# Batch sums moved to earlier steps, and a subtraction of hidden blocks moved from VectorE to GpSimd, in a Strassen-like feed-forward kernel

## The chip, the cores and the metric

The kernel runs on one core of a Trainium2 chip. The metric is device time in microseconds (us) of one execution, the median of several. Engines are called as in the profile: PE (TensorE, matrix products), PEld (its weight loads), DVE (VectorE), ACT (ScalarE), POOL (GpSimd) and SP (SyncE, which only issues transfers here). Each takes its own queue of instructions in order; they meet by semaphores.

## The reference, cut to what matters

```python
# x: (8, 8, 512, 64), state: (8, 8, 32, 64); attention both ways
scores = x @ state^T / sqrt(D);  xread = softmax(scores) @ state
scores2 = state @ x^T / sqrt(D); sread = softmax(scores2) @ x
x = concat([xread, sread], axis=2)       # to (B*(512+32), 512) = (4352, 512)
# feed-forward with w_in (512, 2048), w_out (2048, 512)
h = x @ w_in
g = h * cos(h)
out = g @ w_out
```

All is float32. The cost lies in the two large products.

## The kernel before, in words

The tokens' read of the state is never formed. Since xread = a @ state, the kernel multiplies state by w_in first (the tiles `sw`, by `products`), and h of a batch's 512 tokens is then a product with `sw` and the softmax weights `aT`, with 256 instead of 512 terms.

Work goes in steps. A step is one tile: a batch b and one of 16 blocks f of 128 of the 2048 hidden columns, 128 columns by 512 tokens (128 steps for 8 batches, then 16 for the state rows). `step` counts through, `s` is the step within a batch. Two batches form a pair, and its 32 steps are four phases of 8: 0 and 1 in the even batch, 2 and 3 in the odd one. The second product (g @ w_out) of a pair is done with seven block products instead of eight, so blocks of g of different phases are added and subtracted from each other before they are used. `sums` (L658) and `sums2` (L667) do this by `minus` (L577), which puts the subtraction on DVE where it is called with `True` and the pair isn't the first, and on POOL otherwise.

The first product, h, is also done with seven products of half size where `seven` says so (batches from 2 on, phases 0 to 2), for two tiles at a time:

- `halves` (L481) makes four sums of the quarters of `aT`, on DVE, into `aS`, once a batch (L488).
- `sw_sums` (L496) makes four sums of quarters of `sw`, on POOL, for each couple of tiles: t1, t2 and t4 into `swS`, the fourth in place in `sw` (L502).
- `hidden_a` (L519) is the first four products on PE: one of `aT` and `sw` as they are, then one with t2, one with the quarter changed in place, one with t1 (all L507). `hidden_b` (L542) is the other three, one with t4. `sums_a` (L537 to L539) and `sums_b` (L552, L553) add the parts into g's buffer on DVE, after a copy by ACT (L529).
- `gate` to `gate4` then compute h * cos(h): ACT L560 rounds, DVE L563 subtracts, ACT L566 is the sine, DVE L573 multiplies and leaves g.

`swS` and `aS` have one buffer each. The PSUM pool of h has two buffers.

The order is written out by hand: each engine takes its instructions in the order in which the loop over steps (L920 on) issues them. In a step t: `hidden_b` and `sums_b`, or `hidden` (two plain products, L471); `hidden_a` of the couple that begins at the next step, where there is one; the parts of the attention of the next batch that `plan` puts here; the gates; `gate4`; `sums(t)`; more parts; the sums of w_out's blocks; at the end `sw_sums` for the couple that begins at step + 2, with `halves` before it when that couple begins a batch; `sums2(t)`; and the second product of the tile three steps back (`LAG = 3`, L617). So `hidden_a` of a couple is issued one step after its `sw_sums`.

Of the kernel before, what the change touches and what calls it, by code (L numbers as in the profile page):

```python
# [21 lines left out]
def kernel(  # L22
# [15 lines left out]
    NF = Dff // P  # L38
# [144 lines left out]
    def fetch(n):  # L183
        nonlocal n_fetched
        while n_fetched < n:
            dst, src = loads[n_fetched]
            if f64:
                m, w = dst.shape[1:]

                at_, c0 = (n_fetched - 2) % 3, 0  # L190
                if n_fetched < 4:
                    at_, c0 = n_fetched // 2, n_fetched % 2 * 2 * m * w
                if n_fetched >= N_LOADS:
                    at_ = 3 + n_fetched - N_LOADS
                raw = raw_at[at_].bitcast(I32)[:, c0:c0 + 2 * m * w]
                raw = raw.rearrange("p (m f) -> p m f", m=m)
                nc.sync.dma_start(out=raw, in_=src.bitcast(I32))
                raws[n_fetched] = raw.rearrange("p m (f w) -> p m f w", w=2)
            else:
                nc.sync.dma_start(out=dst, in_=src)  # L200
            n_fetched += 1
# [49 lines left out]
    class Attention:  # L251
# [126 lines left out]
        def sums(self):  # L378
            self.reduce1([self.z1[:, j] for j in range(2)], ALU.add)
            self.inverse(self.m1 if self.b == 0 else self.i12)  # L380
# [72 lines left out]
    def part(b, name, *args):  # L453

        if b not in attn:
            attn[b] = Attention(b)
        getattr(attn[b], name)(*args)
        if (name, args) == ("reads", (1,)) and b + 1 < B:
            if b > 0:
                attn[b + 1] = Attention(b + 1)  # L460
                attn[b + 1].load_tokens()
            load_x(b + 1)
# [16 lines left out]
    def seven(t):  # L479
        return t.pair is not None and t.b > 1 and t.phase < 3  # L480

    def halves(b):
        aT = aT_of[b]
        b11, b12 = aT[:, 0, 0:HS], aT[:, 0, HS:S]
        b21, b22 = aT[:, 1, 0:HS], aT[:, 1, HS:S]
        for i, x1, x2 in ((0, b12, b11), (1, b22, aS[:, 0]), (2, b22, b12),
                          (3, b21, aS[:, 1])):
            nc.vector.tensor_tensor(aS[:, i], x1, x2, op=ALU.subtract)  # L488

    def blocks_of(t):  # L490
        sw = sw_of[t.b, P * t.f // WC]
        c = P * t.f % WC
        return [sw[:, j, c + P * r:c + P * r + P] for r in range(2)
                for j in range(2)]

    def sw_sums(t):  # L496
        b11, b12, b21, b22 = blocks_of(t)
        t1, t2, t4 = [swS[:, i] for i in range(3)]
        sub = ALU.subtract
        for o, x1, x2, op in ((t1, b21, b22, ALU.add), (t2, t1, b11, sub),  # L500
                              (t4, b12, t2, sub), (b21, b11, b21, sub)):
            nc.gpsimd.tensor_tensor(o, x1, x2, op=op)  # L502
# [6 lines left out]
    def take_slot(t):  # L509
        t.slot = g_free.pop(0)  # L510
        t.hp = t.g = g_all[:, t.slot, 0:t.n]

    def both(i1, i2):

        d = i2 - i1
        ends = slice(i1, i2 + (1 if d > 0 else -1), d)
        return g_all.rearrange("p t (h s) -> p (t h) s", h=2)[:, ends]
# [31 lines left out]
    def sums_b(t):  # L549
        e, o = 2 * t.slot, 2 * t.second.slot  # L550
        add = nc.vector.tensor_tensor
        add(t.g[:, LO], t.g[:, LO], t.h1[:, LO], op=ALU.add)  # L552
        add(both(o, e + 1), both(o, e + 1),  # L553
            t.h2.rearrange("p (h s) -> p h s", h=2), op=ALU.add)
# [14 lines left out]
    def gate4(t):  # L569
        if not hasattr(t, "slot"):  # L570
            t.slot = g_free.pop(0)
            t.g = g_all[:, t.slot, 0:t.n]
        nc.vector.tensor_tensor(t.g, t.hp, t.q, op=ALU.mult)  # L573
# [3 lines left out]
    def minus(pr, out, a, b, soon=False):  # L577
        engine = nc.vector if soon and pr.n else nc.gpsimd
        engine.tensor_tensor(out, a, b, op=ALU.subtract)  # L579
# [78 lines left out]
    def sums(t):  # L658
        pr, i = t.pair, t.i
        pr.b[t.phase, i] = t  # L660
        if t.phase == 2:
            minus(pr, pr.b[0, i].g, t.g, pr.b[0, i].g, True)
        if t.phase == 3:
            minus(pr, pr.b[0, i].g, t.g, pr.b[0, i].g, True)
            minus(pr, pr.b[2, i].g, t.g, pr.b[2, i].g)
# [99 lines left out]
    def tiles():  # L765
        pr = None
        for b in range(B):
            if b % 2 == 0:
                pr = Pair(b // 2, pr)
            for f in range(NF):  # L770
                t = Tile()
                t.b, t.f, t.pair = b, f, pr
                t.phase, t.i = b % 2 * 2 + f // NH, f % NH
                t.n, t.kn = S, 2
                c = slice(P * f % WC, P * f % WC + P)
                t.lhs = lambda i, b=b, nt=P * f // WC, c=c: (
                    sw_of[b, nt][:, i, c])
                t.rhs = lambda i, b=b: aT_of[b][:, i]
                yield t
        for n in range(NF):  # L780
            t = Tile()
            t.b, t.n_th, t.f = B, n, (n + NH) % NF
            t.pair, t.last_pair, t.phase = None, pr, None
            t.n, t.kn = B * Ns, NK
            cols = slice(P * t.f, P * t.f + P)
            t.lhs = lambda i, cols=cols: w_in[:, i, cols]
            t.rhs = lambda i: sT[:, :, Ns * i:Ns * i + Ns]
            yield t
# [130 lines left out]
    all_tiles = list(tiles())  # L919
    for step, t in enumerate(all_tiles):  # L920
        s = step % NF
        if s == 0 and t.b < B:
            steps = plan(t.b)
        todo = [p[s] if t.b < B else [] for p in steps]

        def go(n):
            for p in todo[n]:
                part(*p)

        last, conv = conv_at.get(step - 1, -1), conv_at.get(step, -1)  # L930
        if step == B * NF + (0 if f64 else 8):
            fetch(N_LOADS + 2)
        if step == 4:
            warm(1, acc[MAIN][0])
        ahead = all_tiles[step + 1:step + 3]
        if seven(t):
            if t.f % 2 == 0:
                hidden_b(t)
                sums_b(t)
        elif step != 1:  # L940
            hidden(t)
        first = len(ahead) > 1 and seven(ahead[0]) and ahead[0].f % 2 == 0
        if first:
            if not seven(t):

                h = t.hp
                take_slot(t)
                nc.scalar.copy(t.g, h)
            hidden_a(*ahead)
        if step == 0:  # L950
            hidden(all_tiles[1])
            warm(3, acc[MAIN][0])
            gate(t)
            gate2(t)
            convert(3, "bcdf")
            convert(4, "1")
            go(0)
        else:
            go(0)
            if step == 5:  # L960
                states(1, acc[SIDE][1])
            if not (seven(t) and t.f % 2):
                gate(t)
            gate2(t)
            if step == 3:
                warm(4, acc[MAIN][0])
                part(0, "products", 1, SIDE)
            if first:
                sums_a(ahead[0])
            go(1)  # L970
            go(3)
            if step == 1:
                convert(4, "bcdf")
            elif last >= 0:
                convert(last, "bcdf")
            if conv >= 0 and not todo[1]:
                convert(conv, "1")
        gate3(t)
        if seven(t) and t.f % 2 == 0:
            gate(t.second)  # L980
        if step == 3:
            part(0, "products_kept", 1, SIDE)
        if later:
            later.pop(0)()
        gate4(t)
        if conv >= 0 and todo[1] and step > 0:
            convert(conv, "1")
        if t.pair is not None:
            sums(t)
        if step == 6:  # L990
            states_kept(1, acc[SIDE][1])
        go(2)
        if conv >= 0:
            convert(conv, "2")
        go(4)
        if step in block_at:
            blocks(*block_at[step])
        for u in all_tiles[step + 2:step + 3]:
            if seven(u) and u.f % 2 == 0:
                if u.f == 0:  # L1000
                    halves(u.b)
                sw_sums(u)
        if t.pair is not None:
            sums2(t)
        while len(line) >= (LAG if step >= 2 * NH else LAG + 1):
            output(line.pop(0))
        line.append(t)
# [32 lines left out]
```

## Time and profile before

| | |
|---|---|
| median of 3 runs | 775.27 us (774.0 to 775.3) |
| profiled execution | 775.59 us |
| its span, first to last instruction | 773.7 us |
| PE busy | 755.5 us, 98% |
| DVE busy | 519.6 us, 67% |
| ACT busy | 316.2 us, 41% |
| POOL busy | 251.1 us, 32% |
| mean granted PE clock | 0.996 of full |

In the views of the profile a line has a start in us, a duration in us, the engine, the line of the kernel, the operation, and output<-input with sizes. `x2` is a number of merged instructions; a float32 product stands as two matmuls. In square brackets stands how long the engine was idle before it and which engine, tile and line released it. A line of the waits reads: who waited <- for whom: us in total, times, longest. The view of stretches gives, for each, its length, the busy time and count of PE, PEld, DVE, ACT and POOL, then the granted PE clock (1.00 is full), the DMA share and GB/s.

### The profile page before, as it was taken

How to read it: one execution, taken by the hardware profiler on the slowest of the kernel's cores; microseconds unless marked ns; L12 is line 12 of the kernel's file. 1: busy time of each engine (PE TensorE's matmuls, PEld its weight loads, DVE VectorE, ACT ScalarE, POOL GpSimd, SP SyncE). 2: the span in 40 equal slices, each digit the busy share in tenths (PEclk: the TensorE clock that was granted, in tenths of full speed). 3: DMA queues.
4: the chain of work that ended last, by engine and by line, in shares of the span. 5: the costliest groups of instructions: out<-in, count | busy, mean ns of one | idle time of the engine just before them, and what ended most of it. 6: DMA issues, size and time to landing. Idle time of an engine off the chain costs nothing.

```text
span 773.7 us, 8418 instructions
## 1 busy us (share of the span) xinstructions
PE 755.5 (98%) x2880; PEld 380.5 (49%) x2880; DVE 519.6 (67%) x858; ACT 316.2 (41%) x523; POOL 251.1 (32%) x262
## 2 busy tenths in 40 slices
PE   8998999999999999999999999999999999999997
PEld 4443444444555554445555554445555554455554
DVE  5778786645896788756886788567877676431431
ACT  3887844422363435333362335332453333212212
POOL 2353278866121210753121111662121105510200
PEclk9999999999999999999999999999999999999999
DMA  8596451050012510340104310330100115000021
GB/s 244 171 276 206 129 90 28 13 96 1 7 21 43 94 25 4 51 87 0 19 10 83 54 28 14 61 62 1 27 1 1 28 28 136 0 0 15 14 42 41
DMA packets 161962, 43.54 MB, mean 56 GB/s; under 512 B 153920, under 2 KB 153920, under 8 KB 161920
## 3 DMA queue, kind: packets, MB, share of 16 engines
q1 hardware_dynamic: 161024, 42.49, 25.2%
q10 hardware_dynamic: 768, 0.39, 0.2%
q8 instruction: 23, 0.38, 0.2%
q0 software_dynamic: 128, 0.13, 0.1%
q14 instruction: 19, 0.16, 0.1%
HBM read 34.08 MB, written 8.91 MB: 56 GB/s over the span
## 4 chain that ended last, share of the span: by engine, by line
PE 82%; DVE 9%; POOL 3%; ACT 3%; issue 1%; DMA 1%; ACTq 0%; SPq 0%; DVEq 0%; POOLq 0%
PE o L617 44%; PE h L507 14%; PE h L471 13%; PE at L319 4%; PE o L737 4%; PE at L409 2%; DVE q L563 1%; POOL g_all L579 1%; DVE g_all L573 1%; ACT q L560 1%; DVE xT L339 1%; PE o L319 1%; POOL swS L502 1%; ACT q L566 1%; DVE i L333 1%
## 5 line engine op out<-in xcount | busy, mean ns | idle before, releaser
L617 PE MATMUL o<-g_all,w_out 128*128 128x512 f32 x512 | 236.4, 598 | 0.3 <-POOL w_out L242 0.3
L617 PE MATMUL o<-g_all,s 128*128 128x512 f32 x384 | 178.9, 602 | 0.0
L579 POOL TENSOR_TENSOR g_all<-g_all 128x512 f32<-128x512 f32 x80 | 113.2, 1436 | 125.2 <-DVE g_all L573 125.2
L617 PEld LDWEIGHTS o<-g_all,w_out 128*128 128x128 f32 x512 | 93.8, 190 | 113.3 <-issue 108.6
L566 ACT ACTIVATE q<-q,halfpi 128x512 f32<-128x512 f32 (+1 forms) x144 | 100.7, 700 | 91.1 <-DVE q L563 90.9
L563 DVE TENSOR_TENSOR q<-q,h 128x512 f32<-128x512 int32 (+1 forms) x69 | 42.9, 622 | 115.6 <-ACT q L560 115.6
L617 PEld LDWEIGHTS o<-g_all,s 128*128 128x128 f32 x384 | 71.5, 192 | 89.2 <-issue 82.9
L471 PE MATMUL h<-aT,sw 128*128 128x512 f32 x224 | 107.0, 601 | 4.8 <-DVE g_all L573 4.3
L560 ACT ACTIVATE q<-g_all 128x512 int32<-128x512 f32 x75 | 46.8, 624 | 143.9 <-DVE g_all L553 143.5
L560 ACT ACTIVATE q<-h 128x512 int32<-128x512 f32 (+1 forms) x69 | 37.7, 546 | 134.3 <-PE h L471 134.2
L563 DVE TENSOR_TENSOR q<-q,g_all 128x512 f32<-128x512 int32 x75 | 54.8, 731 | 30.8 <-ACT q L560 30.8
L471 PEld LDWEIGHTS h<-aT,sw 128*128 128x128 f32 x224 | 41.8, 190 | 60.0 <-issue 45.1
L502 POOL TENSOR_TENSOR swS<-sw 128x128 f32<-128x128 f32 x36 | 17.7, 492 | 150.0 <-PE h L507 110.6
L573 DVE TENSOR_TENSOR g_all<-g_all,q 128x512 f32<-128x512 f32 x75 | 52.9, 706 | 14.4 <-ACT q L566 14.3
L573 DVE TENSOR_TENSOR g_all<-h,q 128x512 f32<-128x512 f32 (+1 forms) x69 | 42.8, 621 | 25.0 <-ACT q L566 24.6
L242 POOL TENSOR_TENSOR w_out<-w_out,s 128x1024 int32<-128x1024 int32 x10 | 23.9, 2395 | 77.5 <-DVE w_out L237 71.3
L502 POOL TENSOR_TENSOR swS<-sw,swS 128x128 f32<-128x128 f32 x36 | 18.9, 524 | 89.6 <-PE h L507 89.1
L507 PE MATMUL h<-aS,swS 128*128 128x256 f32 x144 | 43.4, 383 | 4.6 <-POOL swS L502 2.4
L507 PE MATMUL h<-aS,sw 128*128 128x256 f32 x144 | 43.2, 382 | 1.4 <-POOL sw L502 1.2
L507 PEld LDWEIGHTS h<-aT,sw 128*128 128x128 f32 x144 | 27.4, 190 | 34.4 <-issue 27.7
L507 PE MATMUL h<-aT,sw 128*128 128x256 f32 x144 | 42.8, 379 | 0.0
L579 DVE TENSOR_TENSOR g_all<-g_all 128x512 f32<-128x512 f32 x48 | 33.4, 696 | 1.6
(103 smaller groups left out, 883.9 us busy)
## 6 DMA issues: line engine op xcount, KB each, us to landing
out_dram<-ot SPq DMA_DIRECT2D x132, 64.0 KB, 2.0
g_all<-in_moe_w_out_dram SPq DMA_DIRECT2D x8, 1024.0 KB, 5.1
g_all<-in_moe_w_in_dram SPq DMA_DIRECT2D x6, 1024.0 KB, 5.4
xT<-in_x_dram SPq DMA_DIRECT2D x96, 64.0 KB, 2.5
x_b<-in_x_dram SPq DMA_DIRECT2D x24, 256.0 KB, 4.4
x_b<-in_x_dram SPq DMA_DIRECT2D x16, 128.0 KB, 3.8
g_all<-in_moe_w_in_dram SPq DMA_DIRECT2D x4, 512.0 KB, 6.2
x_b<-in_moe_w_out_dram SPq DMA_DIRECT2D x1, 1024.0 KB, 5.5
```

Source lines behind the costliest of these rows:

```text
L242: nc.gpsimd.tensor_tensor(bits, bits, e, op=ALU.add)
L319: nc.tensor.matmul(out=(to or at)[j][Ns * k:Ns * k + Ns, 0:n], lhsT=w[D * j:D * j + D, self.b, Ns * k:Ns * k + Ns], rhs=r(slice(D * j, D * ...
L471: nc.tensor.matmul(out=t.hp, lhsT=t.lhs(i), rhs=t.rhs(i), start=(i == 0), stop=(i == t.kn - 1))
L502: nc.gpsimd.tensor_tensor(o, x1, x2, op=op)
L507: nc.tensor.matmul(out=out, lhsT=w, rhs=r, start=True, stop=True)
L560: nc.scalar.activation(t.q.bitcast(I32), t.hp, func=ACTF.Copy, bias=0.25)
L563: nc.vector.tensor_tensor(t.q, t.q.bitcast(I32), t.hp, op=ALU.subtract)
L566: nc.scalar.activation(t.q, t.q, func=ACTF.Sin, bias=halfpi, scale=-TWO_PI)
L573: nc.vector.tensor_tensor(t.g, t.hp, t.q, op=ALU.mult)
L579: engine.tensor_tensor(out, a, b, op=ALU.subtract)
L617: nc.tensor.matmul(out=acc[bank][ch], lhsT=w[:, i, P * ch:P * ch + P], rhs=g.g, start=(i == 0), stop=(i == NH - 1))
L737: nc.tensor.matmul(out=acc[MAIN][i], lhsT=t.g[:, P * i:P * i + P], rhs=w_out[:, :, t.f, :], start=(t.n_th == 0), stop=(t.n_th == NF - 1))
```

## The change

Four places change. `halves` of an odd batch (b > 1) is issued in step 14 of the even batch, right after `sums_b`, where it was at the end of that step. `halves` of an even batch is issued at the end of step 11 of the batch before, where it was at the end of step 14. `sw_sums` of the first couple of an even batch is issued in step 13, ahead of `gate4` and `sums` of that step, where it was at the end of step 14. And `minus` of phase 2 loses its `True`, so that in all pairs it goes to POOL.

```diff
+    def new_pair(t):
+        return t.b % 2 == 0 and t.f == 0
+
...
         if t.phase == 2:
-            minus(pr, pr.b[0, i].g, t.g, pr.b[0, i].g, True)
+            minus(pr, pr.b[0, i].g, t.g, pr.b[0, i].g)
...
             if t.f % 2 == 0:
                 hidden_b(t)
                 sums_b(t)
+                if s == NF - 2 and seven(all_tiles[step + 2]):
+                    halves(t.b + 1)
...
         if later:
             later.pop(0)()
+        for u in all_tiles[step + 3:step + 4]:
+            if seven(u) and new_pair(u):
+                sw_sums(u)
         gate4(t)
...
         go(4)
+        for u in all_tiles[step + 5:step + 6]:
+            if seven(u) and new_pair(u):
+                halves(u.b)
         if step in block_at:
             blocks(*block_at[step])
         for u in all_tiles[step + 2:step + 3]:
-            if seven(u) and u.f % 2 == 0:
-                if u.f == 0:
-                    halves(u.b)
+            if seven(u) and u.f % 2 == 0 and not new_pair(u):
                 sw_sums(u)
```

## The prediction

> **What bounds the kernel now.** I read the busy table first, then TensorE's waits, then the timeline around each wait, then the granted clock in narrow windows. Busy share:
>
> ```profile
> PE 755.5 (98%) x2880; PEld 380.5 (49%) x2880; DVE 519.6 (67%) x858; ACT 316.2 (41%) x523; POOL 251.1 (32%) x262
> ```
>
> TensorE (PE) is busy 98% of the 773.7 us span, so an edit can gain only what PE's waits hold, and costs what new waits it makes. PE's waits (us in total, times, longest), those of the seven-product matmuls at L507:
>
> ```profile
> PE h L507 <- POOL swS L502: 2.4, 3, 1.5
> PE h L507 <- DVE aS L488: 2.2, 3, 0.7
> PE h L507 <- POOL sw L502: 1.2, 3, 0.5
> ```
>
> 5.8 us in all: POOL's `sw_sums` at the start of each even batch (2, 4, 6), DVE's `halves` at the start of each odd one (3, 5, 7). PE's timeline at batches 2, 3 and 4:
>
> ```profile
> 168.93 0.59 PE L507 MATMUL h<-aT,sw 128*128 128x256 f32 x2
> 171.00 0.70 PE L507 MATMUL h<-aS,swS 128*128 128x256 f32 x2 [1.47 <-POOL swS L502]
> 171.95 0.70 PE L507 MATMUL h<-aS,sw 128*128 128x256 f32 x2 [0.25 <-POOL sw L502]
> 172.48 0.61 PE L507 MATMUL h<-aS,swS 128*128 128x256 f32 x2
> ...
> 258.51 0.67 PE L507 MATMUL h<-aS,swS 128*128 128x256 f32 x2 [0.73 <-DVE aS L488]
> ...
> 342.40 0.70 PE L507 MATMUL h<-aS,swS 128*128 128x256 f32 x2 [0.46 <-POOL swS L502]
> ```
>
> The four products of a `hidden_a` start 0.43 us apart when nothing is missing, 1.30 from first to fourth. In batch 2 it is 168.93 to 172.48 = 3.55: 2.25 lost, more than the idle column says. The clock after that wait (columns: stretch, us, five busy times, PEclk, DMA):
>
> ```profile
> 172.90:176.30 3.40, 3.40 (x6) 1.54 (x5) 2.81 (x5) 1.00 (x2) 0.56 (x2) 0.50 0.00 0
> ...
> 342.00:346.00 4.00, 3.11 (x11) 1.84 (x12) 3.02 (x6) 2.01 (x5) 2.69 (x4) 1.00 0.03 6
> ```
>
> After 1.72 us of idle in batch 2, PE ran 3.4 us at half clock: 1.7 us more lost. After 0.95 us in batch 4 it didn't. A 1.95 us wait at 73 us was also followed by about 3.4 us at 0.50. So a PE wait of over some bound between 0.95 and 1.72 us costs a further 1.7.
>
> [...] POOL's first sum at 341.12 starts just as the `minus` ahead of it ends (339.39 + 1.77). [...] Here L579 takes a median of 1.28 us on POOL and 0.69 on DVE.
>
> **Part 1: the even batches' sums sooner.** `halves` goes from the end of step 14 of the batch before (between L573 and L563 in DVE's queue) to the end of step 11; `sw_sums` goes to step 13, ahead of six `minus` of POOL. As built, POOL's order is so. That wait goes: 2.25 + 1.7 of clock in batch 2, and in batches 4 and 6 (341.35 to 344.13, 510.90 to 513.68: 2.78 - 1.30) 1.48 each: 6.9 us. Late next would be ScalarE's copy that frees the second h buffer: L948 ends at 342.19, the third product would start at 342.21; nothing. The cost: the first `minus` of step 13 waits for the copies of sw (L445 ends near 332.2) and four sums (2.0), so till 334.2 instead of 333.67. Its reader comes three steps later. POOL is idle 2.7 us before its next, and the 1.6 us of `halves` at step 11 meets DVE idling over 2 us per step (3.14 before the L563 at 330.72). Without that cover they'd cost some 0.5 and 1.6, three times. No DMA moves, no queue of SP is passed.
>
> **Part 2: the odd batches' `halves` sooner**, right after `sums_b` of step 14. PE's group in batch 3 takes 257.19 to 259.45 = 2.26: 0.96 lost, three times 2.9 us. `halves` (257.49 to 259.04, 1.55) now stands ahead of L563 of step 14, which waits 0.75 for ScalarE's L560 anyway: gate and g of that tile come 0.8 later, read three steps on. Nothing. Parts 1 and 2 together: -9.8 us.
>
> **Part 3: phase 2's `minus` from DVE to POOL**: 24 instructions (8 in each of batches 3, 5, 7). DVE sheds 24 x 0.69 = 16.6 us, no gain: DVE isn't the bound. POOL has 24 x 1.4 = 34 us more, of which it has plenty idle. The cost is order. In an even step t of phase 2, POOL's queue now has `minus(t)`, then the four `sw_sums` of tile t+2. `minus(t)` waits for g of tile t (L573), which ends the whole chain behind `hidden_b(t)`: sums, L560, L563, L566, L573. The four sums wait behind it; their readers are the second to fourth products of `hidden_a(t+2)`, and everything else of PE stands behind those. Now POOL does the last sums straight after `hidden_b`. Batch 3, step 0:
>
> ```profile
> 264.29 0.59 PE L507 MATMUL h<-aS,sw 128*128 128x256 f32 x2
> 265.02 0.46 POOL L502 TENSOR_TENSOR sw<-sw 128x128 f32<-128x128 f32 x1
> 267.95 0.69 DVE L573 TENSOR_TENSOR g_all<-g_all,q 128x512 f32<-128x512 f32 x1 [0.27 <-ACT q L566]
> 268.52 0.59 PE L507 MATMUL h<-aS,sw 128*128 128x256 f32 x2
> 268.68 0.69 DVE L579 TENSOR_TENSOR g_all<-g_all 128x512 f32<-128x512 f32 x1
> ```
>
> The sums are ready at 265.48, PE wants the last at 268.52: 3.0 us spare. After the change they can start only once L573 (268.64) and `minus` are done. I take 0.08 for the hop (346.84 + 0.69 to 347.61), 1.4 for `minus` (1.27 to 1.77 seen) and 2.0 for four sums (1.95 by the pitch of undisturbed ones, 2.42 beside a busy DVE): 3.48, bounds 3.3 and 4.3. So ready at 272.12: 3.6 late, and 0.15 for the restart: 3.75. Since hidden_b, chain and the next hidden_a all move with PE, each stall adds and the next comes again. Step 2: L573 ends 277.93, ready 281.41, wanted 278.41: 3.15. Step 4: L573 ends 288.52, less some 0.4 because DVE's `minus` no longer delays L552: 288.1, ready 291.6, wanted 289.51: 2.25. Step 6 has no reader (tile 8 isn't of the seven kind). Batch 3: 9.15, batch 5 repeats it, batch 7 (607.76, 617.05, 627.0 against 607.64, 617.53, 628.63): 8.9. Sum 27.2 us.
>
> And the clock: idle of about 3.3, 2.7 and 1.8 us within each stall, over or at the 1.72 that halved it. A full 3.4 us at half clock costs 1.7; where the slow stretch falls partly in the stall itself, less. I take 1.5, 1.3 and 0.7: 3.5 a batch, 10.5 in all (0 to 15).
>
> **Sum.** 27.2 + 10.5 - 9.8 = +27.9. The profiled execution took 775.59 (773.7 span and 1.9 around it): 803.5. The median, 775.27, is 0.3 below it, which I let stand.
>
> **The rivals.**
> - A, forecast: new waits with clock drops, 803.5.
> - B: the same waits, but the clock holds[...]: 775.6 + 17.4 = 793. For it: 0.95 in two pieces was harmless. Against: 1.72 in two pieces wasn't.
> - C: POOL at its slow prices (4.3 instead of 3.48, 9 x 0.8 = 7) and a full drop everywhere (15.3 - 10.5 = 5): 815. For it: L502 took 0.9 in places. Against: DVE mostly idles while PE waits, and it is beside each other that the two are slow: `halves` took 1.37 and 1.48 instead of 0.42 beside POOL's `minus` at 167 us.
> - D, the other side: g of tile t comes early enough for `minus` and sums to fit before `hidden_a(t+2)` and only the gain stays, 775.6 - 9.8 = 766. It decides where L573 ends 3.5 us before PE's need; now it ends 0.1 before it in step 0, 0.5 in step 2 and 1 in step 4. DVE freed of 0.69 doesn't bring 2.5. With only step 0 late (3 x 5.3) it would be +6, 782.
> - E: the change doesn't do what it says. As built, the order of POOL and DVE shows all three moves, PE's order is unchanged. I give it nothing.
>
> **How the numbers follow.** A 0.72, B 0.12, C 0.09, D 0.04, its mild form at 782 0.03. The range runs from below B, for the low prices of POOL, to C: 790 to 815; beyond lie D and part of C. About 0.2% can be told from no change here. Faster 0.04 (D), within 0, slower 0.96 (A, B, C and the mild form).
>
> **What would show it.** Right: waits of L507 on POOL in batches 3, 5 and 7, nine groups of 2 to 4 us, sum over 20; the waits on L488 and those at batches 2, 4, 6 gone; PEclk of 0.5 for some 3.4 us after most stalls, mean clock from 0.996 to about 0.97; `minus` 104 on POOL and 24 on DVE; in phase 2 each first sum of a POOL group starting as a `minus` ends. Wrong: PE's first product of `hidden_a` in these batches waiting for nothing, L573 of an even tile ending 3 us earlier against `hidden_b` than now, or stalls under 1 us.

## The result and the profile after

The changed kernel takes 803.78 us (median of 4 runs, 802.15 to 806.69) against 774.67 us before (4 runs on the same chip): 1.038 times as long, 95% interval 1.034 to 1.042. The profiled execution took 802.24, its span is 800.4, 26.7 more than before. The forecast was 803.5. That it is so near is partly luck: of the terms of the sum the largest, the stalls, was right to 1 us, and three others were wrong by 2 to 6 us each and cancelled.

Its page, busy time first:

```profile
span 800.4 us, 8434 instructions
...
PE 761.4 (95%) x2880; PEld 381.2 (48%) x2880; DVE 514.3 (64%) x834; ACT 315.2 (39%) x523; POOL 277.1 (35%) x286
```

PE's busy time rose only by 6 us of the 27: it waits. Its waits (us in total, times, longest):

```profile
PE h L512 <- POOL swS L507: 22.2, 10, 3.1
PE h L471 <- DVE g_all L578: 4.8, 4, 1.9
PE h L512 <- POOL sw L507: 2.2, 9, 0.2
...
PE o L622 <- DVE held L635: 1.4, 2, 0.7
...
PE h L512 <- ACT g_all L955: 0.2, 1, 0.2
```

(Lines are numbered anew: L507 is the sums of `sw`, L512 the seven products, L578 the end of the gate, L584 `minus`, L493 `halves`, L622 the second product, L635 DVE's copy of a finished second product, L955 ScalarE's copy that frees a buffer of h, L910 the sums of w_out's blocks.) The waits on `halves` are gone, those on POOL went from 3.6 to 24.4 us. POOL's timeline in batch 3, at the step whose timeline the prediction shows:

```profile
265.69 1.64 POOL L584 TENSOR_TENSOR g_all<-g_all 128x512 f32<-128x512 f32 x1 [13.25 <-DVE g_all L578]
267.29 0.45 POOL L507 TENSOR_TENSOR swS<-sw 128x128 f32<-128x128 f32 x1
267.82 0.45 POOL L507 TENSOR_TENSOR swS<-swS,sw 128x128 f32<-128x128 f32 x1
268.35 0.46 POOL L507 TENSOR_TENSOR swS<-sw,swS 128x128 f32<-128x128 f32 x1
268.77 0.45 POOL L507 TENSOR_TENSOR sw<-sw 128x128 f32<-128x128 f32 x1
```

and PE's, same stretch:

```profile
264.62 0.59 PE L512 MATMUL h<-aT,sw 128*128 128x256 f32 x2
268.33 1.22 PE L512 MATMUL h<-aS,swS 128*128 128x256 f32 x2 [3.11 <-POOL swS L507]
269.34 1.15 PE L512 MATMUL h<-aS,sw 128*128 128x256 f32 x2
```

POOL was idle for 13.25 us, and the sums could have been made within that time: the first thing in its queue was `minus`, and that waited for DVE's L578, which ended at 265.61. `minus` takes 1.64, the sums 1.93, and PE stands. The products then take 1.22 and 1.15 instead of 0.59: the clock had been halved inside the wait, as the view of the stretches has it (PEclk is third from the end):

```profile
268.00:271.40 3.40, 3.07 (x7) 2.27 (x8) 0.44 (x2) 0.99 (x2) 1.14 (x3) 0.50 0.00 0
```

PE issues the same 2880 products in the same order in both kernels, so the start of the k-th product in one trace can be set against the start of the k-th in the other, and each step in the difference, from level to level, is a gain or a loss at its place:

| where | predicted | found in the two traces |
|---|---|---|
| batch 2, first couple: wait and clock | -2.25 - 1.7 | -1.75 - 1.7 |
| batch 2, second couple | 0 | +1.4 |
| batches 4 and 6 | -1.48 each | -1.29 each |
| batches 3, 5, 7, `halves` | -0.96 each | -0.97 each |
| phase 2, step 0 (three times) | 3.75 each | 3.9 each |
| step 2 | 3.15 each | 3.3 each |
| step 4 | 2.25 (2.0 in batch 7) | 2.2 each |
| clock in those stalls | 10.5 | 1.0 + 1.7 + 1.55 = 4.3 |
| phase 3 of batches 3 and 5 | 0 | +0.95 each |
| sum | +27.9 | +26.7 |

### The profile page after: what moved, and what is told of

Same layout as the page of the kernel before. It is cut to its first block, busy times and chain, and to the rows that moved or that the text cites. A ratio compares the mean times of both kernels' runs of the same rounds, so it can differ in the third digit from the quotient of the medians.

```text
span 800.4 us, 8434 instructions
## 1 busy us (share of the span) xinstructions
PE 761.4 (95%) x2880; PEld 381.2 (48%) x2880; DVE 514.3 (64%) x834; ACT 315.2 (39%) x523; POOL 277.1 (35%) x286
## 4 chain that ended last, share of the span: by engine, by line
PE 75%; DVE 10%; POOL 6%; ACT 4%; issue 4%; DMA 1%; DVEq 0%; SPq 0%; POOLq 0%; ACTq 0%
PE o L622 39%; PE h L471 13%; PE h L512 13%; PE o L742 3%; PE at L319 3%; POOL g_all L584 3%; POOL swS L507 2%; DVE g_all L578 2%; PE at L409 2%; DVE g_all L584 1%; DVE q L568 1%; ACT q L571 1%; DVE xT L339 1%; PE o L319 1%; ACT q L565 1%
## 5 line engine op out<-in xcount | busy, mean ns | idle before, releaser
L622 PE MATMUL o<-g_all,w_out 128*128 128x512 f32 x512 | 238.9, 604 | 0.3 <-POOL w_out L242 0.3
L584 POOL TENSOR_TENSOR g_all<-g_all 128x512 f32<-128x512 f32 x104 | 140.4, 1363 | 197.6 <-DVE g_all L578 190.1
L622 PE MATMUL o<-g_all,s 128*128 128x512 f32 x384 | 177.9, 598 | 1.4 <-DVE held L635 1.4
L622 PEld LDWEIGHTS o<-g_all,w_out 128*128 128x128 f32 x512 | 95.1, 192 | 114.4 <-issue 109.5
L622 PEld LDWEIGHTS o<-g_all,s 128*128 128x128 f32 x384 | 70.7, 190 | 90.2 <-issue 82.8
L568 DVE TENSOR_TENSOR q<-q,g_all 128x512 f32<-128x512 int32 x75 | 52.8, 704 | 35.4 <-ACT q L565 35.4
L512 PE MATMUL h<-aS,swS 128*128 128x256 f32 x144 | 45.3, 397 | 22.2 <-POOL swS L507 22.2
L578 DVE TENSOR_TENSOR g_all<-g_all,q 128x512 f32<-128x512 f32 x75 | 54.3, 724 | 14.4 <-ACT q L571 14.4
L578 DVE TENSOR_TENSOR g_all<-h,q 128x512 f32<-128x512 f32 (+1 forms) x69 | 42.8, 621 | 24.5 <-ACT q L571 24.0
L507 POOL TENSOR_TENSOR swS<-sw 128x128 f32<-128x128 f32 x36 | 17.3, 480 | 107.0 <-PE h L512 66.9
L512 PE MATMUL h<-aS,sw 128*128 128x256 f32 x144 | 45.1, 395 | 2.4 <-POOL sw L507 2.2
L512 PEld LDWEIGHTS h<-aT,sw 128*128 128x128 f32 x144 | 27.4, 190 | 34.4 <-issue 28.2
L512 PE MATMUL h<-aT,sw 128*128 128x256 f32 x144 | 42.8, 379 | 0.0
L512 PEld LDWEIGHTS h<-aS,swS 128*128 128x128 f32 x144 | 27.3, 195 | 29.7 <-POOL swS L507 26.2
L507 POOL TENSOR_TENSOR swS<-sw,swS 128x128 f32<-128x128 f32 x36 | 18.3, 507 | 60.8 <-PE h L512 59.6
```

Source lines behind the costliest of these rows:

```text
L512: nc.tensor.matmul(out=out, lhsT=w, rhs=r, start=True, stop=True)
L568: nc.vector.tensor_tensor(t.q, t.q.bitcast(I32), t.hp, op=ALU.subtract)
L622: nc.tensor.matmul(out=acc[bank][ch], lhsT=w[:, i, P * ch:P * ch + P], rhs=g.g, start=(i == 0), stop=(i == NH - 1))
```

## The experiments

All times are medians beside runs of the kernel before on the same chip, which were 774.1 to 775.4. The runs stand on several chips, so a difference of under 1 us between two of them says little. My theory: the whole loss is the order in POOL's queue, `minus` ahead of sums that are due sooner. The rivals: POOL has too much work, or gets in DVE's way; moving the sums has a cost of its own; the parts work only together.

**The moved sums without the move to POOL.** The changed kernel with

```diff
-            minus(pr, pr.b[0, i].g, t.g, pr.b[0, i].g)
+            minus(pr, pr.b[0, i].g, t.g, pr.b[0, i].g, True)
```

> The change with phase 2's minus left on DVE: only the moved halves and sw_sums. Theory (the cost lies in POOL's queue order alone): no waits of PE at the changes of batches, and no new ones in phase 2 of batches 3, 5, 7; from the shifts of PE between the two traces -3.5 in batch 2 (1.2 given back at its second couple), -1.15 each in batches 4 and 6, -0.75 to -0.93 in batches 3, 5, 7: 767.5 us (766 to 769). Rival (moving the sums costs too, they take DVE's or POOL's time from the gates): 774 or more.

Measured 767.12 us, 0.990 of before (0.989 to 0.992). Parts 1 and 2 are a gain, 7.7 us; the rival is out.

**The move to POOL alone.** The kernel before with the opposite edit of that one line.

> The kernel before with phase 2's minus on POOL and nothing else. Theory: all of the loss and none of the gain: stalls of 27.5, phase 3 up by 1.8, four to seven clock drops of 1.5: 810 us (806 to 815). Rival (the loss comes from the two parts together, as PE runs ahead of POOL once its early waits are gone): well under 800.

Measured 807.97 us, 1.044 (1.042 to 1.046). The loss needs nothing of the other parts: 33.1 us alone, 36.7 on top of them, with different numbers of stretches at half clock, of which more below.

**The same work on POOL, in another order.** The changed kernel with

```diff
+        for u in all_tiles[step + 2:step + 3]:
+            if t.phase == 2 and seven(u) and u.f % 2 == 0:
+                sw_sums(u)
         gate4(t)
...
-            if seven(u) and u.f % 2 == 0 and not new_pair(u):
+            if (seven(u) and u.f % 2 == 0 and not new_pair(u)
+                    and t.phase != 2):
                 sw_sums(u)
```

> The changed kernel with all 24 minus on POOL, but in phase 2 the four sums of the next couple are issued ahead of gate4 and minus, so they stand before it in POOL's queue. Theory (order): the nine stalls go, what is left is e1 and phase 3's 1.8: 769.3 us (768 to 771). Rival (POOL has too much to do, or gets in DVE's way): 790 or more, as POOL does the same work.

Measured 769.98 us, 0.993 (0.992 to 0.995): all but 2.9 us of the loss (803.78 to 767.12) is gone with the same 24 `minus` on POOL. Its timeline at the same place of batch 3:

```profile
260.52 0.45 POOL L507 TENSOR_TENSOR swS<-sw,swS 128x128 f32<-128x128 f32 x1 [3.48 <-PE h L512]
260.93 0.46 POOL L507 TENSOR_TENSOR sw<-sw 128x128 f32<-128x128 f32 x1
264.63 1.66 POOL L584 TENSOR_TENSOR g_all<-g_all 128x512 f32<-128x512 f32 x1 [3.24 <-DVE g_all L578]
```

The sums are done at 261.4, 3.2 us before `minus` may even start, and `minus` starts 1.06 us after PE's first product of the group, where it did so 1.07 after it in the changed kernel. So POOL's load and its meeting with DVE are not the cause of the stalls; the order is. What PE still waits for in this kernel:

```profile
PE h L471 <- DVE g_all L578: 4.7, 4, 1.9
PE at L799 <- DVE g_all L119: 1.5, 1, 1.5
PE o L622 <- DVE held L635: 1.4, 2, 0.7
PE h L512 <- POOL swS L507: 1.0, 1, 1.0
```

The 1.0 is that at batch 2's second couple, the L635 that of phase 3; both come below.

**Half of it each.** `i` is the tile within its phase, so its oddness is the step's.

```diff
-            minus(pr, pr.b[0, i].g, t.g, pr.b[0, i].g)
+            minus(pr, pr.b[0, i].g, t.g, pr.b[0, i].g, i % 2 == 0)   # odd moved
+            minus(pr, pr.b[0, i].g, t.g, pr.b[0, i].g, i % 2 == 1)   # even moved
```

> The changed kernel with only the odd tiles' minus of phase 2 on POOL (12 of 24); the even ones stay on DVE. Theory: an odd tile's minus has no sums of its own step behind it and is done before the next couple's may start, so nothing stalls; phase 3 keeps at most half of its loss: 768.5 us (767 to 770). Rival (each minus on POOL costs alike): half of the loss, about 785.

> The changed kernel with only the even tiles' minus of phase 2 on POOL (12 of 24). Theory: all nine stalls and their clock drops: 803 us (800 to 807). Rival (each minus costs alike): about 785.

Measured 768.06 us (0.991, 0.989 to 0.992) with the odd ones moved, 802.26 (1.035, 1.032 to 1.039) with the even ones. Twelve instructions of the same kind and length on the same engine: 1 us over the kernel with none moved, or 35. Only the even ones stand ahead of sums in their own step.

**Products that fill the wait.** The changed kernel with, in `hidden_a`,

```diff
         product_of(t.h1[:, LO], b11, aT_of[t.b][:, 0, LO])
+        for _ in range({2: 3, 4: 2, 6: 1}.get(t.f, 0) if t.phase == 2 else 0):
+            nc.tensor.matmul(out=t.h2, lhsT=ident, rhs=w_in[:, 0, 0:WC],
+                             start=True, stop=True)
```

(their results are overwritten).

> The changed kernel with products that nothing reads (3, 2 and 1 of 0.86 us) behind the first product of hidden_a in steps 2, 4 and 6 of phase 2, inside the wait. Theory (the spread of 802 to 807 is the number of clock drops that the stalls set off): the stalls stay (27.5), no drop in batches 3, 5, 7: 797.8 us, runs within 1 us of each other. Rival (the drops cost nothing beyond the wait, or the spread has another cause): 803 or more, with a spread of 4.

Measured 797.99 us (1.029, 1.028 to 1.031), four runs from 796.58 to 798.58. In batch 3 PE is kept busy, and the next product starts 3.71 us after the first, as it did in the changed kernel:

```profile
263.16 0.59 PE L512 MATMUL h<-aT,sw 128*128 128x256 f32 x2
263.59 2.74 PE L529 MATMUL h<-w_in,ident 128*128 128x512 f32 x6
...
266.87 0.70 PE L512 MATMUL h<-aS,swS 128*128 128x256 f32 x2 [0.54 <-POOL swS L507]
```

Its trace has no half clock in the batches (its mean clock is 0.999, and PEclk is 1.00 from 264 to 272 us and from 278 to 286). PE was given more work and the kernel became 5.8 us faster. Set against the changed kernel's trace, PE gains 1.0, 1.7 and 1.55 us at the three stalls that had half clock there, 1.3 in batch 0, where no filler stands and the drop is missing too, and nothing elsewhere. So the gain is the price of the clock drops, and 4.3 of it is that of the drops in the stalls. The changed kernel's own runs say the same. From the granted clock and the span, the number of 3.41 us stretches at half clock is (1 - clock) x span / 1.705:

| run, us | clock | span | stretches |
|---|---|---|---|
| 802.15 | 0.991 | 800.2 | 4.2 |
| 802.24 | 0.991 | 800.4 | 4.2 |
| 805.32 | 0.987 | 803.4 | 6.1 |
| 806.69 | 0.985 | 804.8 | 7.1 |

Three more stretches, 4.5 us more: 1.5 each. In these four runs the spread goes with the number of clock drops. (In the four runs with filled waits, 2.0 us apart, it does not: the slowest of them, 798.58, has a clock of 1.000.)

Which wait sets one off shows in part. In the changed kernel's trace the half-clock stretches of batches 3 and 5 last 3.413 us each and start at 267.97, 448.87 and 462.53: 180.90 and 13.66 us apart, 53 and 4 times that length. So I cut each of the thirteen traces into windows of that length, placed by its own half-clock stretches, and counted PE's idle time in each window at full clock after the first 12 us. All 11 windows with over 2.5 us idle were followed by half clock, and none with under 1.7; of the 17 with 1.71 to 1.95 eight were, and why those is open. The same stall of 2.55 us at step 2 lay whole in one window in batch 5 (459.11 to 462.53), and the clock fell; in batch 3 a boundary at 281.62 cut it, the windows had 1.6 and 1.2 us idle, and it did not. That the clock goes by such windows is my reading of these counts; no run tested it by itself.

**Batch 2's second couple.** The kernel with `minus` on DVE, and

```diff
-        if step in block_at:
-            blocks(*block_at[step])
         for u in all_tiles[step + 2:step + 3]:
             if seven(u) and u.f % 2 == 0 and not new_pair(u):
                 sw_sums(u)
+        if step in block_at:
+            blocks(*block_at[step])
```

> The changed kernel with phase 2's minus on DVE, and besides with the sums of w_out's blocks behind sw_sums in a step, not ahead. Theory: the wait at batch 2's second couple (1.02 + 0.24 and the restart), which came to light once PE was 3.5 us earlier there, is POOL's block sum of 2.4 us ahead of sw_sums; it goes, 1.2 us off: 766.0 us. Rival (PE then finds the next late thing at once, or the third couple's sums stand behind the block sum instead): 767.1, as without it.

Measured 765.6 us, 0.987 (0.986 to 0.989), 1.5 below the kernel without it; against that kernel's trace PE gains 1.8 at batch 2's second couple and nowhere else after batch 0. What stood ahead of the sums there, in the changed kernel:

```profile
177.62 2.86 POOL L910 TENSOR_TENSOR w_out<-w_out 128x1024 f32<-128x1024 f32 x1
180.44 0.91 POOL L507 TENSOR_TENSOR swS<-sw 128x128 f32<-128x128 f32 x1
...
182.26 0.70 PE L512 MATMUL h<-aS,swS 128*128 128x256 f32 x2 [1.02 <-POOL swS L507]
```

**Phase 3.** In the changed kernel DVE and POOL start their `minus` of phase 3 (L584) together, as here:

```profile
326.59 1.26 POOL L584 TENSOR_TENSOR g_all<-g_all 128x512 f32<-128x512 f32 x1 [0.80 <-DVE g_all L578]
326.62 1.79 DVE L584 TENSOR_TENSOR g_all<-g_all 128x512 f32<-128x512 f32 x1
328.33 0.68 DVE L635 TENSOR_SCALAR held<-o 128x512 f32<-128x512 f32 x1
```

The kernel before, at the like place:

```profile
315.24 0.69 DVE L579 TENSOR_TENSOR g_all<-g_all 128x512 f32<-128x512 f32 x1
315.29 1.78 POOL L579 TENSOR_TENSOR g_all<-g_all 128x512 f32<-128x512 f32 x1 [2.35 <-DVE g_all L573]
```

In the pairs of either kernel that start within 0.05 us of each other, whichever started first ran at its usual 0.69 or 1.27, and the other took 1.77 to 1.80. In the changed kernel POOL is first in 12 of the 24 tiles, the first four of each batch; in the others DVE's is still first or alone, at 0.69. DVE's reads what POOL's `minus` of phase 2 wrote, and in just these 12 DVE takes a semaphore instruction of 0.02 us ahead of it, starts 0.10 after L578 instead of 0.03 (once 0.46), and so comes second. With only the odd tiles moved that instruction stands at the odd ones of the first four, with only the even ones moved at the even ones. L635, which frees the bank of PE's next product (PE waited for it twice, 1.4 us in all), stands behind DVE's `minus`. To turn the order round, the changed kernel with

```diff
             minus(pr, pr.b[0, i].g, t.g, pr.b[0, i].g, True)
-            minus(pr, pr.b[2, i].g, t.g, pr.b[2, i].g)
...
             minus(pr, pr.b[1, i].g, pr.b[1, i].g, pr.b[0, i].g)
+            minus(pr, pr.b[2, i].g, t.g, pr.b[2, i].g)
```

> The changed kernel with phase 3's two subtractions on POOL in the other order: the one that needs DVE's result first. Theory for the 0.9 us lost in phase 3 of batches 3 and 5: DVE's minus now starts 0.03 us behind POOL's and takes 1.79 instead of 0.69; if POOL's first waits for DVE's, DVE's is back at 0.69 and PE's wait on L635 goes: 1.8 us off, 802.0 against the changed kernel's 803.8, with DVE's 24 minus at a mean of 0.7. Rival (DVE was late because the stalls bunch up its work): DVE's minus stays over 1 us, or it is 0.7 and PE waits as before.

Measured 797.98 us, 1.032 (1.028 to 1.035), 5.8 below the changed kernel where I had written 1.8. DVE's 24 take 0.72 on average, not 1.23:

```profile
L584 DVE TENSOR_TENSOR g_all<-g_all 128x512 f32<-128x512 f32 x24 | 17.3, 720 | 1.7
```

and the wait on L635 is gone. Set against the changed kernel's trace, phase 3 of batches 3 and 5 gives 1.24 each, and two shifts of 0.23 in batches 4 and 6 may belong to it: 2.5 to 2.9 us. The remaining 3 are clock drops: this profile has two of them in the stalls where that of the changed kernel has three and one in batch 0. Runs of the two kernels with like numbers of stretches lie 3.8 apart (4.2 of them: 802.2 and 798.42) and 3.5 (7.1: 806.69 and 803.19). So the mechanism is shown, and its size is between 2.5 and 3.8.

**The two gains alone.** Part 1 alone is the changed kernel with `minus` on DVE and the odd batches' `halves` put back; part 2 alone is the kernel before with

```diff
                 sums_b(t)
+                if s == NF - 2 and seven(all_tiles[step + 2]):
+                    halves(t.b + 1)
...
-                if u.f == 0:
+                if u.f == 0 and u.b % 2 == 0:
                     halves(u.b)
```

> Part 1 alone: halves and sw_sums sooner for batches 2, 4, 6; the odd batches' halves and phase 2's minus as in the kernel before. Theory: the shift of PE in the kernel without the move to POOL gives -3.5 in batch 2 with 1.2 given back at its second couple and -1.35 each in batches 4 and 6: 5.0 off, 770 us. Rival (the parts lean on each other: PE sooner at one change of batches only waits at the next): 772 or more.

> Part 2 alone: the odd batches' halves right after sums_b of step 14; the rest as in the kernel before. Theory: -0.7 to -0.9 three times, 2.5 off: 772.4 us. Rival (the 1.55 of halves ahead of the gate of tile 14 is paid back by later tiles): 774 or more.

Measured 771.28 (0.996, 0.994 to 0.997) and 772.52 (0.997, 0.996 to 0.998). Part 2 is as expected. Part 1 gives 3.1, not 5.0: its median lies between the 770 of the theory and the 772 of the rival. In the traces the two add up: part 1 alone has the same steps as both together (-3.47 and +1.4 in batch 2, -1.3 each in batches 4 and 6), part 2 alone -0.97 in each of batches 3, 5 and 7. In the medians, 3.1 and 1.9 fall short of the 7.7 of both. Part of that is the clock: four of part 1's five runs have one clock stretch (0.998), four of the five with both parts have none. With one stretch each (771.28 and 768.99) part 2 adds 2.3 to part 1, without any (770.08 and 767.1) 3.0, where alone it gave 1.9 in the medians and 2.9 in its profile. What is left, about 1 us, stays open.

Part 2 alone also shows what the clock does with the same wait. In its profile the old waits of 1.47 and 0.25 us stand in batch 2 as before, and then:

```profile
172.90:176.30 3.40, 3.40 (x11) 1.65 (x10) 2.97 (x5) 1.00 (x2) 0.56 (x2) 1.00 0.00 0
```

Full clock, where the kernel before had 0.50 behind the same wait in the same stretch. And PE, 1.7 us sooner for it, then waits at the second couple, +1.6. So the half clock there had cost the kernel before next to nothing.

**All three orders mended, `minus` on POOL.** The edits of the sums first, of phase 3 and of the block sums together.

> The changed kernel, all 24 minus of phase 2 on POOL, with the three orders mended at once: sw_sums ahead of gate4 and minus in phase 2, POOL's minus in phase 3 behind the one that needs DVE's result, w_out's block sums behind sw_sums. Theory (every us of the loss was order, and DVE's relief is worth nothing): the same as the kernel with minus on DVE and the block sums behind, 765.6 us (764.6 to 766.6). Rivals: DVE's relief of 17 us is worth something, under 764.5; or POOL's extra work still costs, 767 or more.

Measured 764.91 us, 0.988 (0.986 to 0.989): as fast as the kernel of batch 2's second couple, with `minus` on DVE (0.987, 0.986 to 0.989). To about 1 us all of the loss was order, and taking 24 instructions off DVE is worth nothing that the medians tell. (The other kernel lacks phase 3's new order. Trace against trace this one gains 1.3 us in five small steps after batch 0, which may come from that order or from DVE's relief; it has a clock drop in batch 0 that the other lacks.) Both are faster than either kernel.

## Why the prediction was right

- *What bounds the kernel.* Right: PE's waits and nothing else.
- *Part 3, the stalls, 27.2.* Right in place and nearly in size: nine stalls, 28.1. `minus` and sums took 3.53 us from POOL's start and 3.61 with the hop, against 3.48. The restart, 0.15 in the working, was 0.06 at batch 3's step 2 (the sum ends at 282.51, PE starts at 282.57), and that product took 0.70 instead of 0.59. (At step 0 the working has L573 end "0.1 before" PE's need; its own lines, 268.64 and 268.52, have it 0.1 after.) Each of the three orders (move alone, sums first, odd or even) bears out that they come from queue order.
- *Part 3, the clock, 10.5.* That the drops cost time is shown by the filled waits, the size is wrong: 4.3 in the profiled run, 5.8 in the medians with batch 0 in it. Half clock followed three stalls of nine, not most, and the mean clock was 0.991, not 0.97. I took a wait of 1.72 us for one that halves the clock. It sometimes is: the same wait in batch 2 was followed by half clock in one kernel and by full clock in two others. In the four profiles with these stalls unfilled (the changed kernel, the move alone, the even ones moved, phase 3 turned round) those of 3.11 + 0.24 set it off 10 times in 12, those of 2.55 + 0.25 twice in 12, those of 1.39 + 0.24 never. I reckoned as if each long wait were hit, and the traces have it vary with where the wait fell: the 2.55 us of step 2 were followed by half clock in batch 5, where one window of 3.413 us held them, and by full clock in batch 3, where two shared them. Part of a slow stretch also falls in the wait itself, where it costs nothing: 0.36 us of that at 267.97.
- *Parts 1 and 2, 9.8.* Right in kind, too large: 7.6 in the traces, 7.7 in the medians. The failed step is "That wait goes: 2.25 + 1.7 of clock in batch 2": 3.47 was gained there and 1.4 came back at once. I asked what is late next within the couple and not at the next couple. There POOL's block sum of 2.86 us stood ahead of `sw_sums`, hidden only because PE came late, by the old wait and the half clock behind it. "Late next would be ScalarE's copy: nothing" was wrong by 0.24 in batch 2, the L955 in the waits; batches 4 and 6 gave 1.29 each, not 1.48.
- *DVE sheds 16.6 us, no gain.* No gain is right. But DVE's busy time fell by 5.3 only, since its 24 `minus` of phase 3 went from a mean of 0.69 to 1.23: I costed the moved instruction and not the wait that it puts on its readers. In phase 3 the kernel lost 1.9 us by it, which the prediction had at nothing. Beside a `minus` of POOL that started first, DVE's took 1.79 us instead of 0.69. I allowed for such meetings in POOL's price (1.27 to 1.77) and not in DVE's.
- *Rivals.* B (the clock holds) is what the filled waits show, 798 for its 793, the 5 us apart being the gain that was over-counted (2.2), phase 3 (1.9) and the stalls (0.9). D needed the end of the gate 3.5 us earlier against PE, and it stayed where it was: at batch 3's step 0, 0.98 us after the first product of the group before and 0.99 after the change.

The errors: stalls +0.9, clock -6.2, gain 2.2 less, phase 3 +1.9. They sum to -1.2 in the profiled run, whose clock drops are fewer than in two of the other three.

## What to carry to other kernels

Before moving an instruction to an engine that is mostly idle, read what stands behind it in that engine's queue and when that is due: a `minus` of 1.64 us that waits for a late result cost 2.2 to 3.9 us each time, and the same one issued behind the sums cost none of that. Ask also what the moved instruction's readers wait for now: a semaphore instruction of 0.02 us in phase 3 made DVE the second of two. When a wait of the bounding engine is taken away, go on to its next two meetings with other engines, as it comes there sooner by what was gained (in batch 2, 1.4 of the 3.47 us gained came back at the second couple). And where a wait of PE is as long as those that half clock followed here (8 of 17 windows with 1.71 to 1.95 us idle, all 11 with over 2.5), reckon its price as a chance, not as a certainty: the same 2.55 us were followed by it in batch 5 and not in batch 3.

## What the runs showed of the hardware

- Work that nothing reads made the kernel faster: filling PE's waits took 5.8 us off, 4.3 of it at the three stalls that had set off half clock, and the spread of runs went from 4.5 to 2.0 us.
- One and the same PE wait (1.47 + 0.25 us) was followed by 3.4 us at half clock in one execution and by full clock in two others. The half clock started 180.90 and 13.66 us apart in the changed kernel's trace (53 and 4 times its own length of 3.413) and 98.99 apart in that of the kernel before (29 times). In windows of that length, placed by each trace's own half-clock stretches, over 2.5 us of PE idle was followed by half clock in 11 of 11, 1.71 to 1.95 in 8 of 17, under 1.7 in none.
- When DVE's and POOL's 128x512 subtractions of two SBUF operands start 0.02 to 0.05 us apart, the first runs at its normal length and the second is stretched: DVE 1.79 instead of 0.69 behind POOL (11 pairs of the changed kernel), POOL 1.77 instead of 1.27 behind DVE (10 pairs there, 22 in the kernel before). In each of them the one held up is the one that started second.
